# First operations of an attention and channel-mix kernel rearranged: loads on other queues, constants on another engine, a new order up to the first mixes

## The chip, the cores and the metric

The kernel runs on one core of a Trainium2 chip. The metric is the time of one execution on the device in microseconds, as a median of several runs. The core has five engines that each work through their own list of instructions in order and wait for one another by semaphores: TensorE (PE in the profile; its weight loads are PEld), VectorE (DVE), ScalarE (ACT), GpSimd (POOL) and SyncE (SP). SP, ACT and POOL also issue DMAs; an issue occupies the place in the issuing engine's list, and the data land later.

## The reference

Two layers in a row, for a batch of 8, 8 heads, 576 positions, head size 64:

```
def phi(x):                                   # x: q or k
    proj = x @ w_phi                          # 64 -> 128 features
    proj = proj - max(abs(proj), axis=-1)
    return concat([exp(proj), exp(-proj)])    # 256 features
q_p, k_p = phi(q), phi(k)
kv  = k_p^T v          ;  z = sum over positions of k_p
att = (q_p kv) / (q_p z + 1e-6)               # linear attention

x  = att, heads side by side                  # 8 x 576 x 512
xk = mu_k * x + (1 - mu_k) * x_prev           # x_prev: the position before
xr = mu_r * x + (1 - mu_r) * x_prev
k  = relu(xk @ w_k)                           # 512 -> 1024
out = sigmoid(xr @ w_r) * ((k * k) @ w_v)
```

Inputs and output are float32; the kernel computes with bfloat16 operands.

## The kernel before

**Tiles.** A batch is four pairs of heads; a pair has a number n from 0 to 31 (batch n // 4). Two heads of 64 partitions each fill the 128 partitions; a partition holds nine consecutive positions, so a pair's k is a tile of 128 x 576, and its q lies behind it in the same tile `nat` (1152 columns, nine groups of 128: groups 0 to 3 are k alone, group 4 is half k and half q, 5 to 8 are q alone).

**The operations, by their names in the code.** A number behind a name is the pair n, for loads and edges the batch and the first pair of the part.

- `hk`, `hq` (DMA issue), then `lk0.0.d`, `lq0.0.d` (cast to bf16): k and q of pair 0. `lk`, `lq`, `lv`: all other loads of k, q and v; k and q are cast by the DMA, which only GpSimd issues. `wphi`, `mus`, `wk`, `wr`, `wv`: the weights.
- `ones`, `ident`, `dve1`, `dve2`, `dve3`: constants. `ident` is the float32 identity (GpSimd); `dve3` makes its bf16 copy and the selection matrices `sel`; `dve1` casts `w_phi`; `dve2` fills thirteen buffers.
- `pt{n}.0`, `pt{n}.1`: transposes of `nat` on TensorE for batches 0 and 1; `pa{n}`, `pb{n}` copy the two halves from PSUM to `qkT`; `tr{n}` is done when both are. Later batches are transposed by DMA.
- `kp`, `qp`: projections on TensorE; `rk`, `rq`: VectorE's reduction to the largest absolute value; `ea`, `eb`: ScalarE's two exponentials of k; `em`: the small exponential of the maxima, which `va`, `vb` multiply into v.
- `mh`, `mt`, `mc`: the maxima of q, split in two bf16 parts, transposed and copied; `qt` makes the transposed projection minus the maximum, `qa`, `qb` its two exponentials.
- `kv`, `kc`: the product of k features and v, and its copy; `nd`: numerator and denominator; `ra`, `rd`: reciprocal and product.
- `xt`, `xe`, `xf`: attention output transposed and copied to `xs`; `df`: difference to the position before; `xa`, `xb`: the mixes with `mu_k` and `mu_r`.
- `tp`, `rt`, `mhe`, `mte`, `mce`, `eme`, `ekt`, `qte`, `eqe`: the same for the ninth group of each pair (the edge), for several pairs at once.
- `h`, `rl`, `sq`, `r`, `th`, `v`, `ob`, `so`: the channel mix of a batch, in eight blocks of `w_k` and four blocks of rows.

**What sets the order.** The string `ORDER` near the top lists all some 1500 operations; the program emits them in that order and every engine executes its own in it. `name:i` names the PSUM buffer (three of two banks, `P0` to `P2`, for most products; two of one bank, `M0` and `M1`, for the channel mix and transposes); `/ENGINE` names the engine where there is a choice; `+m@j` puts m filler matmuls of the constant `ones` into PSUM buffer j ahead of the operation, so that TensorE is not idle. Waits between engines follow from the data.

Batch 0 and most of batch 1's attention come first. The channel mix of batch 0 begins with `h0.0`, which needs the four mixes `xa0` to `xa3`; from there TensorE alternates between the channel mix of one batch and the attention of the next. The beginning of `ORDER` before:

```
ones hk hq ident dve2 hk.d hq.d wphi wphi.d lk0.1 lk0.1.d lq0.1 lq0.1.d mus mus.d lk0.2 lk0.2.d dve3
lq0.2 lq0.2.d lv0.0/POOL lv0.0.d lk0.0.d/DVE lq0.0.d/ACT lv0.1/SP lv0.1.d pt0.0:0+9@0 lv0.2/SP
lv0.2.d pt0.1:1 pa0/DVE pb0/ACT tr0 dve1 tp0.0:0+1@2 kp0:1 rt0.0 qp0:2 rk0 eme0.0 mhe0.0/POOL ekt0.0
```

Of the kernel before, what the change touches and what calls it, by code (L numbers as in the profile page):

```python
# [8 lines left out]
FP = mybir.dt.float32  # L9
# [10 lines left out]
ones hk hq ident dve2 hk.d hq.d wphi wphi.d lk0.1 lk0.1.d lq0.1 lq0.1.d mus mus.d lk0.2 lk0.2.d dve3  # L20
lq0.2 lq0.2.d lv0.0/POOL lv0.0.d lk0.0.d/DVE lq0.0.d/ACT lv0.1/SP lv0.1.d pt0.0:0+9@0 lv0.2/SP
lv0.2.d pt0.1:1 pa0/DVE pb0/ACT tr0 dve1 tp0.0:0+1@2 kp0:1 rt0.0 qp0:2 rk0 eme0.0 mhe0.0/POOL ekt0.0
pt1.0:1+1@0 lk1.0 lk1.0.d pa1/ACT mte0.0:0 rq0 ea0 lq1.0 lq1.0.d pt1.1:1+2@2 pb1/DVE tr1 lk1.2
lk1.2.d eb0 kp1:2+2@2 tp0.1:0 lq1.2 lq1.2.d rt0.1 em0 rk1 qp1:1+1@1 ekt0.1 mh0/POOL eme0.1 wk.0
wk.0.d mt0:1+1@1 mc0/ACT mce0.0/DVE rq1 ea1 qt0:0+1@2 wk.1 wk.1.d wk.d pt2.0:1 qa0 pt2.1:0
mhe0.1/DVE mh1/POOL pa2/DVE pb2/DVE tr2 eb1 vb0/POOL pt3.0:1+2@3 pt3.1:0 pa3/DVE qb0 pb3/DVE tr3
va0/POOL mte0.1:1+1@3 qp2:2 mt1:0 rq2 qp3:1 mce0.1/ACT mc1/ACT em1 qte0.1:1 wr.0 wr.0.d qt1:0 eqe0.1
qte0.0:0 rq3 lv1.0/POOL lv1.0.d qa1 tp0.2:2 va1/POOL qb1 rt0.2 kp2:1+3@1 rk2 vb1/POOL ekt0.2
kv0:0+1@1 eqe0.0 pt4.0:1 kc0/DVE ea2 mhe0.2/POOL pt4.1:0 pa4/DVE kp3:0 pb4/DVE tr4 kv1:2 wr.1 wr.1.d
wr.d eb2 rk3 pt5.0:0 wv.0 wv.0.d pt5.1:1 eme0.2 qp4:1 pa5/DVE kc1/ACT mh2/POOL em2 rq4 nd0:2  # L30
mh3/POOL pb5/ACT tr5 wv.1 wv.1.d wv.d em3 mt2:0 pt6.0:1 ea3 mc2/DVE ra0 nd1:1 vb2/POOL pa6/DVE rd0
eb3 pt6.1:0 pt7.0:1 va2/POOL pb6/DVE tr6 qt2:2 pa7/ACT ra1 rd1 mte0.2:0 qa2 lk2.0 lk2.0.d pt7.1:1
mce0.2/DVE qp5:0 pb7/DVE tr7 qte0.2:0 lq2.0 lq2.0.d qb2 rq5 tp1.0:1 xt0:1 va3/POOL eqe0.2 kv2:2
rt1.0 xf0/ACT xe0/ACT kp4:0 mh4/POOL mt3:0 kc2/ACT rk4 xt1:1 df0/POOL mc3/ACT ekt1.0 nd2:2 ra2 ea4
vb3/POOL xe1/DVE qt3:1+1@0 rd2 mt4:0 xf1/ACT mc4/ACT df1/DVE qa3 xt2:1 xa0 kv3:2 eb4 mhe1.0/DVE
xe2/DVE mte1.0:0+1@0 xb0 kc3/ACT kp5:0 qb3 qt4:2 xa1 eme1.0 xf2/DVE nd3:1 rk5 mce1.0/ACT df2/POOL
qa4 ra3 qb4 rd3 lv1.2/POOL lv1.2.d ea5 xa2 xt3:0+7@1 qp6:2 xb1 qte1.0:1 xe3/ACT qp7:1 eb5 xf3/DVE
df3/DVE xa3 em4 qt5:0+1@0 eqe1.0 rq6 vb4/POOL h0.0:0 qa5 va4/POOL rq7 kp6:2 qb5 h0.1:1 rk6 mh6/POOL
kp7:1 rl0.1/ACT kv4:0 va5/POOL rl0.0/ACT tr2.0 tr2.0.d tr8 tr9 mt6:1 kc4/DVE ea6 h0.2:0 rk7 vb5/POOL
eb6 xb2 kv5:0+1@2 mc6/ACT sq0.0/ACT xb3 nd4:2 tr2.2 tr2.2.d tr10 tr11 em6 ea7 h0.3:1 kc5/DVE  # L40
vb6/POOL ra4 rd4 nd5:0 eb7 vb7/POOL rl0.3/DVE qt6:2 rl0.2/ACT ra5 qp8:1 rd5 qa6 lv2.0/SP lv2.0.d
sq0.1/POOL r0.0:1 rq8 qb6 va6/POOL qp9:0 h0.4:0 rq9 th0.0 sq0.3/POOL sq0.2/ACT qt7:2 kv6:1 rl0.4/DVE
qa7 lk3.0 lk3.0.d tp2.0:0 kc6/DVE h0.5:1 mh8/POOL rt2.0 qb7 va7/POOL xt4:0 rl0.5/ACT kp8:1 xf4/DVE
xe4/DVE qp10:2 eme2.0 lq3.0 lq3.0.d r0.1:1 rk8 ekt2.0 mhe2.0/POOL r0.2:0 th0.1 rq10 sq0.4/POOL ea8
kp9:0 h0.6:1 rk9 lv2.2/POOL lv2.2.d eb8 kv7:2 th0.2 df4/DVE qp11:1 sq0.5/DVE rl0.6/ACT h0.7:0 xa4
em8 sq0.6/ACT kc7/DVE va8/POOL mt8:1 rq11 rl0.7/ACT nd6:2 mc8/ACT ea9 mte2.0:0 vb8/POOL xt5:1 ra6
nd7:1 rd6 tr3.0 tr3.0.d tr12 tr13 mce2.0/ACT eb9 vb9/POOL qte2.0:0 ra7 kv8:2 rd7 xf5/ACT sq0.7/ACT
qt8:0 va9/POOL kc8/DVE eqe2.0 kp10:1 xe5/DVE kp11:2 rk10 v0.0:1 tr3.2 tr3.2.d tr14 tr15 df5/POOL qa8
rk11 ea10 lk4.0 lk4.0.d v0.1:0 qb8 mh10/DVE xa5 lv3.0/SP lv3.0.d eb10 xb5 kv9:0 xb4 em10 qt9:1
kc9/ACT ob0.0 va10/POOL nd8:0 qa9 ob0.1 v0.2:1 qb9 vb10/POOL ra8 rd8 ea11 lq4.0 lq4.0.d mt10:0  # L50
tp3.0:0 ob0.2 kv10:1 mc10/ACT vb11/POOL eb11 rt3.0 so0.2 so0.2.d xt6:0 xt7:1 kc10/ACT va11/POOL
kp12:2 xf7/ACT xf6/DVE qt10:1 xe6/DVE ekt3.0 xz8 xz8.d xe7/DVE r0.3:0 df6/DVE qa10 rk12 df7/POOL
nd9:0 qb10 v0.3:1 ra9 mhe3.0/POOL rd9 th0.3 xa6 ea12 xz9 xz9.d mte3.0:0 qt11:0 xa7 eb12 nd10:1
mce3.0/DVE ob0.3 tr4.0 tr4.0.d tr16 tr17 h1.0:0 qa11 xb6 h1.1:1 qb11 ra10 xb7 kv11:2 rl1.0/ACT rd10
kp13:0 eme3.0 tr4.2 tr4.2.d tr18 tr19 sq1.0/POOL qte3.0:0 kc11/DVE rl1.1/ACT qp12:1 rk13 qp13:2
# [12 lines left out]
xz13 xz13.d qt16:1 kc15/ACT v1.3:1 xb11 ea17 tr5.2 tr5.2.d tr22 tr23 sqe0.0/DVE eb17 xa10 nd15:0
xa11 eme4.0 ve0:0 em16 ra15 ob1.3 qa16 va16/POOL so1.2 so1.2.d rd15 qb16 h2.0:1 va17/POOL obe0 xz14
xz14.d qp18:0 rl2.0/ACT qte4.0:0 vb16/POOL rq18 qp19:1 xz15 xz15.d eqe4.0 qp20:2 h2.1:1 sq2.0/POOL  # L70
rq19 so1.3 so1.3.d h2.2:0 rl2.1/ACT vb17/POOL rq20 sq2.1/ACT h2.3:1 lv4.2/SP lv4.2.d rl2.2/ACT soe0
soe0.d kp18:1 xb10 rl2.3/ACT kv16:2 sq2.3/ACT df12/DVE qp21:0 h2.4:1 xb12 sq2.2/ACT rq21 r2.0:0
rl2.4/ACT r2.1:1 th2.0 mh18/DVE kc16/DVE mh20/POOL xu13/ACT rk18 lk6.0 lk6.0.d kv17:0 th2.1 tp5.0:2
sq2.4/ACT lq6.0 lq6.0.d mt18:0 h2.5:1 rt5.0 kc17/ACT mc18/ACT df13/POOL ea18 mt20:0 nd16:0 mc20/DVE
rl2.5/DVE ekt5.0 h2.6:0 mhe5.0/POOL ra16 rd16 h2.7:1 eb18 sq2.5/DVE xz16 xz16.d xa13 qt17:0
rl2.6/ACT qt18:1 rl2.7/ACT sq2.6/DVE kp19:2 qa17 sq2.7/DVE r2.2:0 xb13 qa18 v2.0:1 xa12 xu14/ACT
rk19 th2.2 df14/POOL qb17 v2.1:0 ob2.0 xu15/ACT xa14 ea19 mte5.0:1 nd17:0 eme5.0 mce5.0/DVE ob2.1
eb19 v2.2:1 df15/DVE ra17 qb18 xa15 em18 qp22:2 ob2.2 qt19:1 vb18/POOL rq22 h3.0:0 tr6.0 tr6.0.d
tr24 tr25 qa19 va18/POOL r2.3:1 qb19 rl3.0/DVE rd17 vb19/POOL kp20:2 th2.3 qte5.0:0 kv18:1 rk20
# [81 lines left out]
def kernel(  # L161
# [17 lines left out]
    nc = tc.nc  # L179
# [102 lines left out]
    st = {}  # L282
# [734 lines left out]
```

## Time and profile before

| what | value |
|---|---|
| time, median of 3 runs | 285.27 us (283.28 to 286.0) |
| span of the profiled execution, first to last instruction | 275.3 us |
| median minus span | 10.0 us |
| TensorE busy | 261.7 us, 95% |
| VectorE busy | 234.6 us, 85% |
| ScalarE busy | 223.1 us, 81% |
| GpSimd busy | 142.4 us, 52% |

The profile lists the span of its execution, and no separate time for it; the runs shown are timed as a whole, and what lies around the span there is 10.0 us against the median. A line of the timeline has the start, the length, the engine, the line of code, the tile written and the tile read, and in brackets how long the engine was idle ahead of it and what ended that. Instructions of one engine overlap by up to about 0.1 us, so the cost of one is best read from its start to the start of the next.

### The profile page before, as it was taken

The page shows a single profiled execution, that of the slowest core. Times are in us where ns is not written, and L with a number is a line of the kernel's source. Part 1 is how long each engine was busy: PE and PEld are TensorE (multiplying, and loading weights), DVE is VectorE, ACT ScalarE, POOL GpSimd, SP SyncE. Part 2 cuts the span into 40 slices and gives each one's busy share as a digit, 9 for nine tenths or more (in the row PEclk, how much of TensorE's full clock was granted, in tenths as well). Part 3 has the DMA queues.
Part 4 walks back from the last instruction along what each step waited for, and adds up shares of the span by engine and source line. Part 5 has one row for each costly group of instructions (what it writes and reads, how often), then busy time and mean ns, then how long its engine had stood idle before and what let it go on. Part 6 is the DMA issues. An engine that isn't in the chain of part 4 may idle for free.

```text
span 275.3 us, 8865 instructions
## 1 busy us (share of the span) xinstructions
PE 261.7 (95%) x3682; PEld 154.1 (56%) x3730; DVE 234.6 (85%) x388; ACT 223.1 (81%) x413; POOL 142.4 (52%) x193
## 2 busy tenths in 40 slices
PE   7899889999899999999999999999999999999993
PEld 3567656566555566555565666555566565444542
DVE  6999999999799989999999889998889897864222
ACT  3899999999899997899898999789987777616330
POOL 5799557976818682633459465821931611300200
PEclk9999999999999999999999999999999999999999
DMA  7999999599999899759699998981725324142134
GB/s 147 285 209 250 209 213 174 114 235 175 238 129 200 202 219 185 155 127 248 99 166 164 215 249 142 171 255 41 161 89 88 77 52 100 42 110 67 29 88 116
DMA packets 65817, 42.89 MB, mean 156 GB/s; under 512 B 47152, under 2 KB 57008, under 8 KB 65776
## 3 DMA queue, kind: packets, MB, share of 16 engines
q1 hardware_dynamic: 54496, 27.54, 49.3%
q0 software_dynamic: 11056, 14.42, 29.1%
q8 instruction: 29, 0.48, 0.8%
q10 hardware_dynamic: 224, 0.36, 0.5%
q14 instruction: 12, 0.10, 0.1%
HBM read 33.62 MB, written 9.44 MB: 156 GB/s over the span
## 4 chain that ended last, share of the span: by engine, by line
PE 75%; DVE 8%; ACT 6%; issue 4%; DMA 3%; POOL 2%; SPq 0%; POOLq 0%; ACTq 0%
PE ps_h L810 19%; PE ps_v L843 17%; PE ps_r L829 9%; PE ps_nd L677 5%; PE ps_kv L656 5%; DMA qkT<-nat 3%; PE ps_he L897 3%; PE ps_ve L929 3%; PE ps_k L566 2%; PE ps_qT L630 2%; PE ps_q L566 2%; PE ps_qT L636 2%; ACT k L605 2%; DVE nmk L579 2%; PE ps_f L292 1%
## 5 line engine op out<-in xcount | busy, mean ns | idle before, releaser
L597 POOL TENSOR_TENSOR v<-vt,v 128x576 bf16<-128x576 f32 x59 | 69.8, 1203 | 33.5 <-ACT v L591 31.1
L605 ACT ACTIVATE k<-ps_k 128x1024 bf16<-128x1024 f32 x64 | 64.8, 1047 | 1.3 <-DVE nmk L579 1.3
L643 ACT ACTIVATE q<-ps_qT 128x1024 bf16<-128x1024 f32 x64 | 63.8, 1054 | 1.8 <-PE ps_qT L636 1.7
L810 PE MATMUL ps_h<-xk,wk_bf 128*128 128x512 bf16 x235 | 60.5, 380 | 1.2
L843 PE MATMUL ps_v<-wv_bf,kk 128*128 128x512 bf16 x244 | 58.2, 379 | 0.6
L579 DVE TENSOR_REDUCE nmk<-ps_k 128x8 f32<-128x1024 f32 x32 | 38.8, 1217 | 1.8 <-PE ps_k L566 1.5
L584 DVE TENSOR_REDUCE nmq<-ps_q 128x8 f32<-128x1024 f32 x32 | 38.3, 1217 | 1.6 <-PE ps_q L566 1.4
L843 PEld LDWEIGHTS <-kk 128*128 128x128 bf16 x256 | 24.1, 98 | 27.3
L810 PEld LDWEIGHTS <-wk_bf 128*128 128x128 bf16 x256 | 22.7, 97 | 25.0 <-issue 0.7
L206 ACT ACTIVATE krelu<-ps_h 128x512 bf16<-128x512 f32 x48 | 28.8, 611 | 9.3 <-PE ps_h L810 9.3
L726 POOL TENSOR_TENSOR diff<-xs 128x576 bf16<-128x576 bf16 x15 | 20.2, 1346 | 28.8 <-ACT xs L706 12.7
L214 POOL TENSOR_TENSOR kk<-krelu 128x512 bf16<-128x512 bf16 x18 | 19.1, 1068 | 30.3 <-ACT krelu L206 26.6
L849 DVE SCALAR_TENSOR_TENSOR ob<-rt,ps_v 128x512 f32<-128x512 bf16 x32 | 21.7, 682 | 14.3 <-PE ps_v L843 12.7
L829 PE MATMUL ps_r<-wr_bf,xr 128*128 128x512 bf16 x116 | 31.1, 380 | 0.7
L835 ACT ACTIVATE rt<-ps_r 128x512 bf16<-128x512 f32 x32 | 19.7, 615 | 8.8 <-PE ps_r L829 8.7
L732 DVE SCALAR_TENSOR_TENSOR xk<-diff,mu_k_t,xs 128x576 bf16<-128x576 bf16 x32 | 26.7, 839 | 0.1
L689 DVE TENSOR_TENSOR x_sc<-ps_nd,rden 128x640 bf16<-128x640 f32 x32 | 26.0, 817 | 0.6
L732 DVE SCALAR_TENSOR_TENSOR xr<-diff,mu_r_t,xs 128x576 bf16<-128x576 bf16 x32 | 25.6, 806 | 0.1
L656 PE MATMUL ps_kv<-v,k 64*128 64x65 bf16 x1024 | 22.4, 190 | 0.5 <-ACT q L643 0.2
L566 PEld LDWEIGHTS <-qkT 64*128 64x128 bf16 x512 | 16.5, 94 | 11.0 <-issue 8.0
L656 PEld LDWEIGHTS <-k 64*128 64x128 bf16 x1024 | 19.3, 94 | 5.7 <-issue 1.8
L677 PE MATMUL ps_nd<-kv,q 128*128 128x65 bf16 x512 | 21.4, 193 | 0.0
(102 smaller groups left out, 414.3 us busy)
## 6 DMA issues: line engine op xcount, KB each, us to landing
out_dram<-ob SPq DMA_DIRECT2D x70, 128.0 KB, 2.5
vt<-in_v_dram SPq DMA_DIRECT2D x11, 576.0 KB, 6.1
nat<-in_k_dram POOLq DMA_DIRECT2D x6, 576.0 KB, 7.8
nat<-in_q_dram POOLq DMA_DIRECT2D x6, 576.0 KB, 8.0
vt<-in_v_dram POOLq DMA_DIRECT2D x4, 576.0 KB, 6.0
wk_bf<-in_moe_w_k_dram POOLq DMA_DIRECT2D x2, 512.0 KB, 11.4
wv_bf<-in_moe_w_v_dram POOLq DMA_DIRECT2D x2, 512.0 KB, 10.6
nat<-in_k_dram POOLq DMA_DIRECT2D x3, 288.0 KB, 6.9
```

The costliest lines, as they stand in the source:

```text
L206: nc.scalar.activation(out_, in_, AF.Relu, scale=HALF)
L579: nc.vector.tensor_reduce(t[:, j, :], s["k"].rearrange("p a (g f) -> p (a g) f", f=128), axis=AX.X, op=ALU.max, apply_absolute_value=True, ...
L584: nc.vector.tensor_reduce(t[:, j, :], s["q"].rearrange("p a (g f) -> p (a g) f", f=128), axis=AX.X, op=ALU.max, apply_absolute_value=True, ...
L597: (nc.vector if eng == "DVE" else nc.gpsimd).tensor_tensor(vb[:, a, pn, :, 0:64], vt[b, a // 2][:, a % 2, :].rearrange("p (s d) -> p s d", ...
L605: nc.scalar.activation(s[f"k{pn}"], s["k"].rearrange("p a (g f) -> p (a g) f", f=128), AF.Exp, scale=(1.0 if pn == 0 else -1.0))
L643: nc.scalar.activation(t.rearrange("f x (a p) -> f x a p", a=2), s["qT"].rearrange("f a (x p) -> f x a p", p=64), AF.Exp, scale=(1.0 if pn ...
L656: nc.tensor.matmul(ps[:, hh, pn * 65:(pn + 1) * 65], lhsT=s[f"k{pn}"][r, c, :], rhs=vb[r, a, pn, 2 * g + par, :], start=(pn == 0 and c == ...
L677: nc.tensor.matmul(ps[:, bk, o * 65:(o + 1) * 65], lhsT=tail if sl < 2 else s[f"q{pn}"][:, 2 * G + h, :], rhs=s["kv"][:, h, pn, :], start= ...
L732: nc.vector.scalar_tensor_tensor(out=t[:, a, (b % 2) * S:(b % 2 + 1) * S], in0=s["d"], scalar=mu[:, a:a + 1], in1=xs[:, a, 0:S], op0=ALU.m ...
L810: nc.tensor.matmul(ps, lhsT=wk_bf[:, c, fc * 128:(fc + 1) * 128], rhs=xkt[bp][:, c, m0:m0 + 512], start=(c == 0), stop=(c == NDC - 1))
L829: nc.tensor.matmul(ps, lhsT=xrt[bp][:, c, m0 + ci * 128:m0 + (ci + 1) * 128], rhs=wr_bf[:, c, :], start=(c == 0), stop=(c == NDC - 1))
L843: nc.tensor.matmul(ps, lhsT=s["kk"][:, fc, ci * 128:(ci + 1) * 128], rhs=wv_bf[:, fc, :], start=(fc == 0), stop=(fc == NFC - 1))
```

## The change

The order is written anew from its first word to about `xf7`; from `r0.3` on it is the same. Up to `xa3` nearly all is in another place. The beginning of `ORDER` after:

```
ones hk wphi wphi.d wphj wphj.d dve2 hk.d ident dve0 lk0.0.d/DVE dve1 pt0.0:0+6@0 pa0/DVE kp0:1+1@2
rk0 hq hq.d lq0.0.d/ACT pt0.1:1 pb0/ACT lk0.1 lk0.1.d pt1.0:0 tr0 mus mus.d lq0.1 dve4 lq0.1.d lk0.2
lk0.2.d tp0.0:0+1@2 qp0:2 pa1/DVE rt0.0 rq0 pt1.1:1+1@0 ea0 ekt0.0 pb1/ACT tr1 kp1:0 qp1:2+1@1
pt2.0:1 dve3 rk1 lq0.2 lq0.2.d lv0.0/POOL lv0.0.d lv0.1/POOL lv0.1.d lk1.0 lk1.0.d lq1.0 mhe0.0/POOL
```

- `w_phi` is loaded in two halves from two queues (`wphi` on ACT's, `wphj` on SP's) in place of twice on SP's. `hq` goes from ACT's queue to SP's, behind `wphj`.
- The bf16 identity has an operation of its own (`dve0`), and the transposes wait for it and not for the rest of `dve3`, which now comes after the first reductions.
- The memsets of `xs` and `tq` (six) go from VectorE to GpSimd (`dve4`), behind the load `lq0.1`.
- The transposes of a pair are split 4 and 5 in place of 5 and 4: the first half holds k alone and waits only for k. The first projection of k (`kp`) waits for the first half alone.
- `mu_k` and `mu_r` are loaded as rows of 128 (two DMAs of 4 x 128), transposed on TensorE (`mut`) and copied by VectorE (`muc`); before, each was loaded column by column as 128 x 4 single elements.
- Both other loads of batch 0's v (`lv0.1`, `lv0.2`) go from SP's queue to GpSimd's.
- Some small operations change the engine: `mhe0.1`, `mhe1.0` from VectorE to GpSimd; `pb1`, `pa2`, `pa3`, `kc0`, `xf2`, `xf3` from VectorE to ScalarE; `pa1`, `pb5`, `mce0.1`, `mc1`, `xf0`, `kc3` from ScalarE to VectorE; `df0` and `df2` from GpSimd to VectorE, `df1` from VectorE to GpSimd.
- There are 29 filler matmuls in place of 36; the first group of them has 6 in place of 9.

```
-    def c_wphi():
-        for hh in range(2):
-            nc.sync.dma_start(out=wph_f32[64 * hh:64 * hh + 64, :], in_=w_phi)
+    def c_wphi(hh):
+        def f():
+            (nc.sync, nc.scalar)[hh].dma_start(out=wph_f32[64 * hh:64 * hh + 64, :], in_=w_phi)
+        return f
...
+    def c_dve0():
+        nc.vector.tensor_copy(ident, ident_f32)
     def c_dve2():
         for t in mhls + mhlts + [zero]:
             nc.vector.memset(t, 0.0)
+    def c_dve4():
         for t in xss:
-            nc.vector.memset(t[:, :, 0:1], 0.0)
+            nc.gpsimd.memset(t[:, :, 0:1], 0.0)
         for t in tqs[0] + tqs[1]:
-            nc.vector.memset(t[:, :, 0:64], 1.0)
+            nc.gpsimd.memset(t[:, :, 0:64], 1.0)
     def c_dve3():
-        nc.vector.tensor_copy(ident, ident_f32)
...
-                for g in range(5 * bk, min(R, 5 * bk + 5)):
-                    nc.tensor.transpose(pb[:, g - 5 * bk, :], nat[b][:, a, g * 128:(g + 1) * 128], ident)
+                for g in ((0, 1, 2, 3), (4, 5, 6, 7, 8))[bk]:
+                    nc.tensor.transpose(pb[:, g - 4 * bk, :], nat[b][:, a, g * 128:(g + 1) * 128], ident)
...
-                nc.scalar.dma_start(out=st["kq"][:, 1, :], in_=heads(q, 0, 0, 1)[:, 0, :])
+                nc.sync.dma_start(out=st["kq"][:, 1, :], in_=heads(q, 0, 0, 1)[:, 0, :])
...
-                    op(f"pt{i}.{bk}", "PE", 0.3, ("pt", i), pt(b, a, bk), [f"lk{tag}.d", f"lq{tag}.d", "dve3"],
+                    op(f"pt{i}.{bk}", "PE", 0.3, ("pt", i), pt(b, a, bk), [f"lk{tag}.d", "dve0"] + [f"lq{tag}.d"] * bk,
...
     def mus():
-        nc.sync.dma_start(out=mu_k_t, in_=moe_mu_k.rearrange("(c p) -> p c", p=128))
-        nc.sync.dma_start(out=mu_r_t, in_=moe_mu_r.rearrange("(c p) -> p c", p=128))
+        for i, mu in enumerate((moe_mu_k, moe_mu_r)):
+            nc.sync.dma_start(out=mu_rows[NDC * i:NDC * i + NDC, :], in_=mu.rearrange("(c p) -> c p", p=128))
+    def mut():
+        st["mu"] = ps = motile(("mo", "mu"), "ps_mu")
+        nc.tensor.transpose(ps[:, 0:2 * NDC], mu_rows, ident_f32[0:2 * NDC, 0:2 * NDC])
+    def muc():
+        nc.vector.tensor_copy(mu_t, st["mu"][:, 0:2 * NDC])
...
-        op("kp" + N, "PE", 0.23, (K("kp"), n), kp, ["tr" + N, "dve1"],
+        op("kp" + N, "PE", 0.23, (K("kp"), n), kp, [("pa" if b < NPT else "tr") + N, "dve1"],
```

## The prediction

> **What bounds the kernel now.** I read the page first, then the windows by stage, then the timelines of ScalarE and VectorE up to the first block of the channel mix.
>
> ```profile
> span 275.3 us, 8865 instructions
> ...
> PE 261.7 (95%) x3682; PEld 154.1 (56%) x3730; DVE 234.6 (85%) x388; ACT 223.1 (81%) x413; POOL 142.4 (52%) x193
> ```
>
> ```profile
> 35.00:40.00 5.00, 4.53 (x55) 2.52 (x53) 4.89 (x9) 5.00 (x10) 2.45 (x3) 1.00 1.11 249
> 40.00:60.00 20.00, 19.06 (x346) 11.39 (x351) 19.84 (x28) 19.65 (x36) 16.59 (x22) 1.00 0.88 159
> ...
> 100.00:150.00 50.00, 49.42 (x740) 28.42 (x747) 47.75 (x74) 43.18 (x80) 27.64 (x36) 1.00 0.92 164
> ```
>
> The columns are TensorE, weight loads, VectorE, ScalarE, GpSimd, clock, DMA share and GB/s. Behind 40 us TensorE is full (49.4 of 50 us). Ahead of it ScalarE and VectorE are full, and TensorE's time is padded with fillers. The new order ends there, so the question is how much earlier `h0.0` and the blocks behind it start (39.61 us here); what is won or lost by then should arrive at the end one to one.
>
> ```profile
> 4.83 0.67 ACT L200 CAST nat<-kk 128x576 bf16<-128x576 f32 x1 [2.37 <-DMA kk<-in_q_dram]
> 6.54 0.59 ACT L200 COPY qkT<-ps_pt 128x512 bf16<-128x512 bf16 x1 [1.03 <-PE ps_pt L338]
> ...
> 8.84 1.95 ACT L605 ACTIVATE k<-ps_k 128x1024 bf16<-128x1024 f32 x2
> ...
> 11.87 0.27 ACT L200 COPY mT<-ps_m 128x128 bf16<-128x128 bf16 x1 [0.34 <-PE ps_m L620]
> ...
> 19.80 1.94 ACT L605 ACTIVATE k<-ps_k 128x1024 bf16<-128x1024 f32 x2 [0.20 <-DVE nmk L579]
> ...
> 39.95 2.06 ACT L643 ACTIVATE q<-ps_qT 128x1024 bf16<-128x1024 f32 x2
> 42.28 1.08 ACT L206 ACTIVATE krelu<-ps_h 128x512 bf16<-128x512 f32 x2 [0.27 <-PE ps_h L810]
> ```
>
> From `ea0` at 8.84 to `qa5` at 39.95 ScalarE is idle for 0.34 + 0.20 us only. Its first `krelu` then waits 0.27 us for TensorE, so ScalarE is not the very last there; VectorE is:
>
> ```profile
> 4.67 0.46 DVE L202 CAST nat<-kk 128x576 bf16<-128x576 f32 x1 [0.62 <-DMA kk<-in_k_dram]
> 6.26 0.49 DVE L202 COPY qkT<-ps_pt 128x640 bf16<-128x640 bf16 x1 [1.13 <-PE ps_pt L338]
> ...
> 8.68 1.22 DVE L584 TENSOR_REDUCE nmq<-ps_q 128x8 f32<-128x1024 f32 x1
> 9.81 0.41 DVE L202 COPY qkT<-ps_pt 128x512 bf16<-128x512 bf16 x1
> ...
> 39.61 2.35 DVE L584 TENSOR_REDUCE nmq<-ps_q 128x8 f32<-128x1024 f32 x2
> ```
>
> `xa3` ends where `rq6` starts, at 39.61. Of these 39.6 us VectorE is busy for 35.5; of the 4.1 idle, 3.0 lie ahead of `rk0` (7.55) and 1.1 behind it.
>
> **The start.** Here the change does most. k's cast begins at 4.67, as its data land 3.9 us after the issue at 0.74; q's ends at 5.50, and only then the transposes begin (5.53), behind nine fillers that last 4.02 us.
> - k's landing: 4.65 as now if its own queue limits it, or about 3.5 if it no longer shares the engines with q (by the DMA rates of the first microseconds 288 KB have moved by 3.2). I take 4.0. Cast 0.46: 4.5. Six fillers (6 x 0.43) end at 4.03. Four transposes (now five in 0.70): 5.1. `dve1` lies ahead of `pa0` on VectorE and waits for both halves of `w_phi`; SP's lands at 1.21 + 3.8 = 5.0, as the first one now, and before the second one now (1.80 + 4.4). `pa0` 0.4: 5.6. `kp0` to `rk0` 0.45, `rk0` 1.13: **7.25, now 8.68**.
> - q is issued third on SP, at 1.80 and not at 0.74. It lands at 5.0 if the bytes decide (the same bytes are ahead of it as now), at 5.9 if 4.1 us from the issue stay; I take 5.3. Cast 0.67, five transposes 0.65, `pb0` 0.69: 7.3. `ea0` is behind it on ScalarE: **7.3, now 8.84**. `tp0.0` and `qp0` need `pb0`, so `rt0.0` starts at 7.7 and `rq0` ends at **9.3, now 9.81**.
>
> The Trainium skill has a rule against fewer fillers. "TensorE: Matmul & The Clock Gate", Part 1, says that the array runs at half its clock until about 3.4 us of sustained activity. The rows: fillers 0.43 us apart up to 4.42, the first five transposes in 0.70 us, later ones in 0.45, so the gate opens near 5.6, some 4.1 us behind the first matmul. (The page's clock row shows 9 throughout and does not show this.) Six fillers are 2.6 us. By the row the gate opens at the same time and only `pt0.0` is slow, which is in the sum; by the rule, with TensorE pausing at 4.0, `kp0` (8) and `pt0.1` (5) are slow too, 13 x 0.053 = 0.7 us on the two paths together. I keep the row; 0.7 goes into the range.
>
> **ScalarE's sum.** Behind `ea0` it has 31.11 - 0.54 = 30.57 us of work up to `qa5`. `eme0.0` (0.20), `ekt0.0` (0.39) and `pb1` (0.58) come behind `ea0` now: +1.17. Engine changes: `pa2`, `pa3` +0.92, `kc0` +0.26, `xf2`, `xf3` +0.20; `kc3` -0.26, `mce0.1`, `mc1` -0.30, `pb5` -0.46, `pa7` (four groups in place of five) -0.19, `xf0` -0.10: +0.07. So 31.8, from 7.3: 39.1, and with the same 0.54 idle **39.65, now 39.95: -0.3 us**. Most of the 1.5 won at `ea0` is work that was done in the gap ahead of it.
>
> **VectorE's sum.** At the end of `rq0` it is 0.5 ahead. But `dve3` without the identity (2.89 to 4.05, 1.16 us) was done in the wait for k and is now among the reductions; `pa1` is done in place of `pb1` (-0.4). The rest of the list: `mhe0.1`, `mhe1.0` -0.54, `pa2`, `pa3` -0.66, `kc0` -0.33, `df1` -0.38, `xf2`, `xf3` -0.30; `pb5` and wider `pb7` +0.47, `kc3` +0.35, `df0`, `df2` +0.76, `mce0.1`, `mc1` +0.26, `xf0` +0.12, `muc` +0.13: -0.12. Together +0.64 - 0.5 = **+0.1 us** at the same 1.1 idle. The six memsets (1.8 to 2.8) also leave VectorE, but they lay in its wait for k; that gains nothing.
>
> **GpSimd and the loads.** `dve4` is not in the trace on GpSimd. Bounds: 1.1 us as on VectorE, or 1.6 by GpSimd's 0.20 for 128 float32 columns (four of 256 at most 0.4); I take 1.4. It is hidden in GpSimd's idle 2.95 us ahead of 7.70, but `lk0.2` behind it is issued at 4.1 and not 2.69, `lq0.2` at 4.85 and not 3.40, and `pt2.0` stands on TensorE at about 10 in place of 12.65. Behind that two v issues (+1.4) and `mhe0.1`, `mhe1.0` (+0.9) against `df0` or `df2` (-1.3) leave it about 1 us more up to `vb3`. Then `vb3` ends near 30, ahead of `kv3` (31.67 now).
>
> ```profile
> nat<-in_k_dram POOLq DMA_DIRECT2D x3, 288.0 KB, 6.9
> nat<-in_q_dram POOLq DMA_DIRECT2D x3, 288.0 KB, 7.8
> ...
> kk<-in_k_dram SPq DMA_DIRECT2D x1, 288.0 KB, 3.9
> ...
> mu_k_t<-in_moe_mu_k_dram SPq DMA_DIRECT2D x1, 2.0 KB, 7.1
> mu_r_t<-in_moe_mu_r_dram SPq DMA_DIRECT2D x1, 2.0 KB, 8.5
> ```
>
> The two `mu` loads are 1024 packets of 4 bytes; while they run the DMA engines stay full and the rate falls from 380 to 60 GB/s (6 us). As rows they are eight packets of 512 bytes, and two v loads leave SP's queue as well. So I let the loads of pairs 1 to 3 land no later than now plus their later issue: `lk0.2` 4.1 + 6.4 = 10.5, `lq0.2` 4.85 + 7.8 = 12.6. `pa2` on ScalarE is due at about 10.7; nothing large is lost. `mut` is one small transpose where TensorE has room. Seven fillers fewer cost nothing where TensorE waits anyway.
>
> **The sum.** ScalarE -0.3, VectorE +0.1 at equal idle. The idle behind `rk0` (0.2, 0.2, 0.3 for TensorE's projections) may shrink by 0.3 to 0.5, as projections stand earlier in the list. I take **-0.3 us: 285.0**, from a span of 275.3 to 275.0 with the 10.0 us around it.
>
> **Rivals.**
> - **The gaps close.** q lands at 5.0 (-0.3), ScalarE loses its 0.54 and VectorE its 1.1. ScalarE then sets it: 39.95 to 38.8, -1.15: **284.1**. For it: both are full but for these gaps, and the small `mu` packets go. Against: each gap has its own cause, and a new order has new ones.
> - **The loads come late (slower).** `pt2.0` and `pt2.1` stand early in TensorE's list and block all behind them. Take the longest landings for 288 KB in the first 13 us, 8.6 for k and 9.3 for q: `lk0.2` lands at 12.7, `pa2` starts at 13.2, and ScalarE is idle 2.5 us: 0.3 less 2.5 is +2.2, **287.5**. It decides from `lk0.2` landing after about 10.5. For it: later issue, earlier use. Against: fewer bytes and packets ahead.
> - **The start is no earlier.** The order does what it says, but k lands at 4.65, q at 5.9 and TensorE is cold: `ea0` at about 8.2, +0.6: **285.9**.
>
> **How the numbers follow.** The forecast has 0.5, closed gaps 0.23, late loads 0.17, no earlier start 0.10. A measurement of this kernel tells about 1% (2.9 us) from no change; the three runs shown spread from -0.7 to +0.3%. Over 1% faster needs more than closed gaps: 0.14, from that case and scatter. Over 1% slower: 0.13, most of the late loads with a second stall. Within: 0.73. The range reaches from closed gaps with scatter, 282.5, to late loads, 287.5.
>
> **What would show it.** Right: `rk0` ends near 7.3, `ea0` starts near 7.3, `rq0` ends near 9.3, ScalarE without idle from there to `qa5` near 39.6; `h0.0` between 39 and 40. Wrong: a ScalarE copy `qkT` between 9 and 14 us with over 1 us of idle behind `ps_pt` (late loads); `h0.0` before 38 (the gaps were worth more, or the sums missed work); or a span that differs by more than `h0.0` does, which would mean that what lies behind 40 us is not the same.

## The result, and the profile after: 1.2% slower, and in the profile a start that is 6 us later

| | before | after |
|---|---|---|
| median of 22 executions each | 284.6 us | 284.19 us |
| lowest and highest | 279.5 to 290.68 us | 281.83 to 297.93 us |
| time against before, as a ratio | 1 | 1.0116, 95% interval 1.0068 to 1.0164 |
| span of the profiled execution | 275.3 us | 281.4 us |
| `h0.0` starts | 39.61 us | 45.64 us |

The ratio leaves out executions that lie more than 1.5% above the fastest of their kernel, and this is why it can show a loss where the medians are equal. What makes so many executions of before long is found below (e8 and e9).

The page of after, cut to the lines that answer to those of before, and the row of the granted clock:

```profile
span 281.4 us, 8854 instructions
...
PE 263.6 (94%) x3675; PEld 154.9 (55%) x3724; DVE 234.8 (83%) x380; ACT 224.0 (80%) x413; POOL 143.8 (51%) x204
...
PEclk9599979999999999999999999999999999999999
```

The work is what it was (VectorE 234.8 us, ScalarE 224.0); the span is 6.1 us longer. The clock row has a 5 and a 7 in its second and sixth slice, where before had 9 throughout. The windows by stage of after (TensorE, weight loads, VectorE, ScalarE, GpSimd, granted clock, DMA share, GB/s) show where:

```profile
4.80:8.20 3.40, 0.66 (x10) 0.22 (x8) 1.65 (x2) 0.40 (x1) 2.93 (x5) 0.97 1.05 167
8.20:11.60 3.40, 3.01 (x25) 2.06 (x26) 1.54 (x3) 2.34 (x5) 0.51 (x3) 0.50 1.13 275
11.60:15.00 3.40, 3.03 (x27) 1.63 (x26) 2.91 (x6) 2.37 (x6) 3.30 (x6) 0.52 1.19 217
...
35.40:38.80 3.40, 2.23 (x53) 1.44 (x54) 2.25 (x5) 3.40 (x6) 1.71 (x2) 0.99 1.16 175
38.80:42.20 3.40, 3.18 (x34) 2.02 (x35) 3.35 (x6) 2.26 (x5) 0.25 (x1) 0.51 1.19 223
...
100.00:150.00 50.00, 49.38 (x727) 29.20 (x732) 47.49 (x76) 44.35 (x83) 24.43 (x34) 1.00 0.93 173
```

From 4.8 to 8.2 us TensorE works for 0.66 us and ScalarE for 0.40. In the two stretches behind it TensorE is busy again, at half the clock, and a second time from 38.8 to 42.2 us (clock 0.51). From 100 to 150 us TensorE is as full as before (49.38 of 50 us, before 49.42), and from `h0.0` to the end both kernels take the same: 281.4 - 45.64 = 235.8 us, before 275.3 - 39.61 = 235.7. The loss of this profile is made ahead of `h0.0`.

What stands still is seen on the timelines of ScalarE and of VectorE:

```profile
7.80 0.67 ACT L200 CAST nat<-kk 128x576 bf16<-128x576 f32 x1 [5.21 <-DMA kk<-in_q_dram]
9.28 0.69 ACT L200 COPY qkT<-ps_pt 128x640 bf16<-128x640 bf16 x1 [0.81 <-PE ps_pt L348]
9.87 1.03 ACT L624 ACTIVATE k<-ps_k 128x1024 bf16<-128x1024 f32 x1
...
46.48 1.05 ACT L662 ACTIVATE q<-ps_qT 128x1024 bf16<-128x1024 f32 x1
```

```profile
3.81 0.46 DVE L202 CAST nat<-kk 128x576 bf16<-128x576 f32 x1 [1.90 <-DMA kk<-in_k_dram]
...
5.81 1.22 DVE L598 TENSOR_REDUCE nmk<-ps_k 128x8 f32<-128x1024 f32 x1 [0.50 <-PE ps_k L585]
9.71 0.42 DVE L202 COPY qkT<-ps_pt 128x512 bf16<-128x512 bf16 x1 [2.68 <-PE ps_pt L348]
...
10.91 1.22 DVE L603 TENSOR_REDUCE nmq<-ps_q 128x8 f32<-128x1024 f32 x1
...
45.74 2.36 DVE L603 TENSOR_REDUCE nmq<-ps_q 128x8 f32<-128x1024 f32 x2
```

k is early: its cast starts at 3.81 (before 4.67) and `rk0` at 5.81 (before 7.55). q is late: its cast starts at 7.80 (before 4.83), and ScalarE has waited 5.21 us for that DMA alone. `pt0.1` needs q, and it stands ahead of `pt1.0` in TensorE's list, so TensorE waits too, and then VectorE for TensorE (2.68). `ea0` starts at 9.87 (before 8.84). The list of DMA issues of the first 6 us (line, queue, kind, count, KB, us to landing) shows which loads lie together:

```profile
kk<-in_k_dram SPq DMA_DIRECT2D x1, 288.0 KB, 3.1
kk<-in_q_dram SPq DMA_DIRECT2D x1, 288.0 KB, 5.9
...
nat<-in_k_dram POOLq DMA_DIRECT2D x1, 144.0 KB, 5.8
nat<-in_q_dram POOLq DMA_DIRECT2D x1, 144.0 KB, 6.3
```

q is issued on SP at 1.84, third on its queue, and takes 5.9 us; on ACT's queue, issued at 0.74 beside k, it took 4.1. The two cast loads of pair 1 (`lk0.1`, `lq0.1`, issued by GpSimd at 1.44 and 2.15) are under way in the same microseconds, and take 5.8 and 6.3 where before they took 4.4 and 5.4. The packets of the two queues from 4.9 to 5.3 us (packets, MB, share of the 16 DMA engines' time; q0 carries GpSimd's cast loads, q1 SP's loads):

```profile
q0 software_dynamic: 32, 0.03, 53.5%
q1 hardware_dynamic: 30, 0.07, 50.2%
```

Here q goes packet for packet with the cast loads, and has half of the engines' time.

The second stretch at half clock delays the mixes as well. The same sixteen products of an `nd` take 1.07 us in after, and 0.67 in e10 below, whose start is the same. First after, then e10:

```profile
38.96 1.07 PE L696 MATMUL ps_nd<-kv,q 128*128 128x65 bf16 x16
```

```profile
37.95 0.67 PE L696 MATMUL ps_nd<-kv,q 128*128 128x65 bf16 x16
```

From the filler ahead of it, at 37.07 (36.78 in e10), to `h0.0` after needs 8.57 us and e10 7.27: 1.3 us of the 6.0 are lost here. Of the nine profiles with the new start, after's and eight below, only after and e1 have this stretch. In the 3.4 us ahead of it TensorE is busy for 2.2 us and never idle for more than 0.55 us at once; what sets it off stays open.

### The profile page after: what moved, and what is told of

Its sections match the earlier page's. It is cut to its first block, busy times and chain, and to the rows that moved or that the text cites. A ratio compares the mean times of both kernels' runs of the same rounds, so it can differ in the third digit from the quotient of the medians.

```text
span 281.4 us, 8854 instructions
## 1 busy us (share of the span) xinstructions
PE 263.6 (94%) x3675; PEld 154.9 (55%) x3724; DVE 234.8 (83%) x380; ACT 224.0 (80%) x413; POOL 143.8 (51%) x204
## 4 chain that ended last, share of the span: by engine, by line
PE 79%; ACT 6%; DMA 5%; DVE 4%; issue 2%; POOL 2%; SPq 0%; ACTq 0%; DVEq 0%; POOLq 0%
PE ps_h L829 19%; PE ps_v L862 18%; PE ps_r L848 10%; PE ps_nd L696 6%; PE ps_kv L675 5%; DMA qkT<-nat 3%; PE ps_he L916 3%; PE ps_k L585 3%; PE ps_qT L649 3%; PE ps_ve L948 3%; PE ps_q L585 2%; PE ps_qT L655 2%; DMA kk<-in_q_dram 2%; DVE nmq L603 2%; ACT k L624 2%
## 5 line engine op out<-in xcount | busy, mean ns | idle before, releaser
L598 DVE TENSOR_REDUCE nmk<-ps_k 128x8 f32<-128x1024 f32 x32 | 38.8, 1218 | 3.7 <-PE ps_k L585 3.2
L745 POOL TENSOR_TENSOR diff<-xs 128x576 bf16<-128x576 bf16 x14 | 18.7, 1338 | 26.9 <-ACT xs L725 12.8
L751 DVE SCALAR_TENSOR_TENSOR xk<-diff,mu_t,xs 128x576 bf16<-128x576 bf16 x32 | 26.6, 839 | 0.1
L751 DVE SCALAR_TENSOR_TENSOR xr<-diff,mu_t,xs 128x576 bf16<-128x576 bf16 x32 | 25.7, 808 | 0.1
```

The costliest lines, as they stand in the source:

```text
L598: nc.vector.tensor_reduce(t[:, j, :], s["k"].rearrange("p a (g f) -> p (a g) f", f=128), axis=AX.X, op=ALU.max, apply_absolute_value=True, ...
L751: nc.vector.scalar_tensor_tensor(out=t[:, a, (b % 2) * S:(b % 2 + 1) * S], in0=s["d"], scalar=mu[:, a:a + 1], in1=xs[:, a, 0:S], op0=ALU.m ...
```

## The experiments

Theory from the two traces: q's late landing and the cold TensorE behind it are the 6 us. Rivals: TensorE's clock alone; the queue that q is on; the new order itself, with gaps of its own. Later a second question came up: why executions of one kernel lie 277 to 290 us apart.

**e1: q on ACT's queue, as before.** In the order:

```
-ones hk wphi wphi.d wphj wphj.d dve2 hk.d ...   -rk0 hq hq.d lq0.0.d/ACT ...
+ones hk hq wphi wphi.d wphj wphj.d dve2 hk.d ...   +rk0 hq.d lq0.0.d/ACT ...
```

and `nc.scalar` in place of `nc.sync` for q.

> The changed kernel, but q of pair 0 is issued first on ACT's queue (ahead of w_phi's half), as before the change. Theory 1 (q's late landing holds TensorE's list at pt0.1): q lands near 4.8 in place of 7.8, ea0 starts near 7.0 in place of 9.9, TensorE's clock stays full behind 8 us, the channel mix begins 3 to 5 us earlier (41 to 43 us), and the span falls by as much, to 276.5 to 278.5. Rival (the new order behind the start is the worse one): ea0 moves as above but the channel mix still begins at 44 us or later and the span stays within 1.5 us of 281.4.

Measured: ratio to before 1.0053 (1.0016 to 1.009), median 281.29 us. The timelines of ScalarE and VectorE of this kernel:

```profile
4.73 0.67 ACT L200 CAST nat<-kk 128x576 bf16<-128x576 f32 x1 [1.67 <-DMA kk<-in_q_dram]
7.63 0.69 ACT L200 COPY qkT<-ps_pt 128x640 bf16<-128x640 bf16 x1 [2.23 <-PE ps_pt L348]
```

```profile
5.73 0.23 DVE L254 CAST wph<-wph_f 128x128 bf16<-128x128 f32 x1 [0.71 <-DMA wph_f<-in_w_phi_dram]
```

q's cast starts at 4.73, 3.1 us earlier, but `pb0` only at 7.63. Now the halves of `w_phi`, one of them behind q on ACT's queue, land at 5.3 and 5.6 (4.0 and 4.1 in after): `dve1` waits for them, `pa0` behind it on VectorE, `kp0` for `pa0`, and `pt0.1` behind `kp0` on TensorE. q in time gives 1.6 us at `ea0` (8.25) and 2.6 at `h0.0` (43.09), not all; the second stretch at half clock is in this trace too (36.35 to 39.77 us).

**e2: q second on SP's queue, `w_phi`'s half third.** Only the order: `hk hq wphi wphi.d wphj wphj.d`, and `rk0 hq.d`.

> The changed kernel, but q of pair 0 is issued second on SP's queue, ahead of w_phi's half and not behind it (0.6 us earlier, same queue). If the place among the loads decides (q comes to the DMA engines before the two cast loads of pair 1), q lands near 5 and the span is as in the run with q on ACT's queue. If SP's queue itself carries one load of k's size at a time, q lands near 7 and half of the loss stays.

Measured: ratio 1.0127 (1.0051 to 1.0203), median 282.1 us. q landed 3.3 us behind its issue, and the half of `w_phi` behind it took 5.0: `pb0` at 8.63, `h0.0` at 43.18. A load of 32 KB in third place is late as one of 288 KB is, and both orders put something there that TensorE's list needs.

**e3: `dve4` ahead of the cast loads `lk0.1` and `lq0.1` on GpSimd.** q stays third on SP.

```
-... hk.d ident dve0 lk0.0.d/DVE ...   lq0.1 dve4 lq0.1.d lk0.2
+... hk.d ident dve4 dve0 lk0.0.d/DVE ...   lq0.1 lq0.1.d lk0.2
```

> The changed kernel, but GpSimd's six memsets come ahead of the two cast loads of pair 1 (lk0.1, lq0.1), which are issued 1.1 to 1.3 us later; q stays third on SP's queue. If q is late because it shares the DMA engines with these two loads, it lands near 5.5 and ea0 starts near 7.7; pair 1 comes later, so the span gains 1 to 3 us. If q is late because of its own queue, it still lands after 7.3.

Measured: ratio 1.003 (0.998 to 1.008), median 280.98 us. The cast loads are issued at 2.31 and 3.02, 0.9 us later than in after. One line of the DMA issues, and two of ScalarE's timeline:

```profile
kk<-in_q_dram SPq DMA_DIRECT2D x1, 288.0 KB, 4.0
```

```profile
5.83 0.67 ACT L200 CAST nat<-kk 128x576 bf16<-128x576 f32 x1 [3.23 <-DMA kk<-in_q_dram]
...
7.63 1.03 ACT L624 ACTIVATE k<-ps_k 128x1024 bf16<-128x1024 f32 x1
```

From the same place on the same queue q takes 4.0 us in place of 5.9. So the place alone is not what costs: it costs when one cast load is issued 0.4 us ahead of q and the next 0.3 us behind it (1.44 and 2.15 against 1.84), and not when both come behind: from 4.0 to 4.5 us SP's queue moves 71 packets beside 9 of the cast loads. The other profiles say the same: with the cast loads as in after q takes 5.9 to 6.1 us (after, e4, e10, e11), with both behind it 3.6 and 4.0 (e12, e3). `ea0` is at 7.63 and `h0.0` at 40.94, 4.7 us earlier than in after, by moving one word in the order; against e10 and e11 below, which have no second stretch at half clock, it is 3.1 and 2.4 us.

**e4: ten more fillers ahead of `pt0.1`** (`pt0.1:1+10@2`), so that TensorE works while q is late.

> The changed kernel with ten filler matmuls more, ahead of pt0.1, so that TensorE is busy while q is awaited. If the half clock from 8 to 15 us is a large part of the loss, the clock stays above 0.9 there and the span falls by 1 to 2.5 us from 281.4. If q's landing alone costs the time, the clock is full but the span stays within 0.7 us of 281.4 (or rises where the fillers are still running when q has landed).

Measured: ratio 1.0069 (1.0022 to 1.0115), median 281.08 us. q's cast is as late as ever (7.78), but `h0.0` starts at 42.55. Two rows of TensorE's timeline in e4, the nine transposes (`pt0.1` and `pt1.0`) and the filler behind them:

```profile
8.51 0.68 PE L348 MATMUL ps_pt<-ident,nat 128*128 128x128 bf16 x9 [0.26 <-ACT nat L200]
9.02 0.38 PE L302 MATMUL ps_g<-ones 128*128 128x512 bf16 x1
```

and the same two in after:

```profile
8.53 1.14 PE L348 MATMUL ps_pt<-ident,nat 128*128 128x128 bf16 x9 [2.77 <-ACT nat L200]
9.47 0.63 PE L302 MATMUL ps_g<-ones 128*128 128x512 bf16 x1
```

The same nine transposes, started within 0.02 us of each other, take 0.68 us in one and 1.14 in the other. A pause of 2.8 us behind 4.3 us of fillers, transposes and products (1.46 to 5.77) makes TensorE slow for what follows. `h0.0` is 3.1 us earlier than in after; 1.4 of these are the second stretch, which e4 does not have (7.17 us from the filler at 35.38 to `h0.0`, 8.57 in after). So the first is worth about 1.7 us here, and 1.5 and 0.8 against e10 and e11.

**e5: e1 and e3 together.**

> The changed kernel with two repairs at once: q of pair 0 first on ACT's queue, and GpSimd's memsets ahead of the cast loads of pair 1. If the late start is what the change lost, k, q and both halves of w_phi land by about 5, ea0 starts at 6.5 to 7.5, the clock stays full, and the channel mix begins at 39.5 to 41 us: a span of 275 to 277, level with the kernel before or faster. If the new order behind the start has more gaps of its own, ea0 starts that early too, but the mix begins 33 us or more behind ea0 (30.8 before the change) and the span stays above 277.

Measured: five of six executions at 290 to 295 us, the sixth at 278.26. At the start q's cast was at 5.17 and k's at 5.00 (both loads, side by side, took 4.2 and 4.4 us), `ea0` at 8.56, `h0.0` at 41.88: no better than e3. Behind it TensorE stood still for 10.76 us in one wait, at about 74 us, for a DMA transpose. That made the second question.

**e6: before, with q on SP's queue behind `w_phi`.** `hk ident dve2 hk.d wphi wphi.d hq hq.d`, and `nc.sync` for q.

> The kernel before, with one part of the change: q of pair 0 is issued last of four on SP's queue, behind both loads of w_phi, and no longer on ACT's. Theory 1: q lands 2 to 3 us later (7 to 8 us), the transposes, which need k and q there, start as late, and the span rises by 2.5 to 6 us, the more so if TensorE's clock falls in the pause. Rival (the place of q costs little, the order is what costs): the span stays within 1 us of 275.3.

Measured: ratio 1.0411 (1.0306 to 1.0516), median 290.07 us. The late q is here as well (cast 7.75, TensorE at a clock of 0.53 from 8.2 to 11.6), and costs the old order 3.5 us at `h0.0` (43.15). Most of the rest is again the wait at 74 us, 9.22 us here.

**e7: before, with `mu_k` and `mu_r` loaded as rows** (`mut`, `muc` as in after, behind `tr3`).

> The kernel before, with mu_k and mu_r loaded as rows, transposed and copied as in the change, and nothing else. If the 1024 packets of 4 bytes slow the other loads, lk0.2 and lq0.2 land 1 us or more earlier than 6.4 and 7.8 us after their issue and the dip of the DMA rate between 5 and 7 us goes; the time stays within 0.5%, as nothing waits for these loads. If the dip has another cause, it stays.

Measured: ratio 1.0173 (0.9955 to 1.0391) from four executions, which tells nothing of the time. The trace tells enough: `lk0.2` and `lq0.2` landed 7.1 and 9.4 us behind their issue, with the packets of 4 bytes 6.4 and 7.8. The loads came no sooner, and `h0.0` was at 39.99.

**e8: before, unchanged, beside e5 to e7.**

> The kernel before, unchanged, with a profile of its own: how far the one profiled execution of before (275.3 us, clock full throughout) stands for its runs. If it does, most undisturbed runs have spans of 275 to 278 and a clock of 1.0; if it was a good draw, they lie at 277 to 281 with clocks below 1.0.

Measured: median 281.78 us, 278.71 to 291.43; ratio to the other executions of the same kernel 1.0074 (0.9965 to 1.0183). `h0.0` at 39.78 as in the profile of before, and a span that is 4.4 us longer. So the profiled execution of before (275.3) was one of its fastest, and 4.2 us of another lie behind `h0.0`.

2.8 of them lie in one wait, and TensorE is at half clock for 3.4 us behind it (75.18 to 78.59). The one that waits is the first product of batch 3's edge (`tp3.0`, tile `ps_e`) and it waits for the second of batch 3's two DMA transposes. Its row in TensorE's timeline, in before, in e8 and in e6:

```profile
71.63 0.29 PE L466 MATMUL ps_e<-wph,qkT 64*128 64x128 bf16 x4 [1.07 <-DMA qkT<-nat]
```

```profile
74.54 0.28 PE L466 MATMUL ps_e<-wph,qkT 64*128 64x128 bf16 x4 [3.82 <-DMA qkT<-nat]
```

```profile
83.75 0.39 PE L466 MATMUL ps_e<-wph,qkT 64*128 64x128 bf16 x4 [9.22 <-DMA qkT<-nat]
```

Four transfers meet here. GpSimd issues `lq3.0` and, 10.3 us later in before, `lk4.0`, whatever happens. SP may start batch 3's first transpose (`tr3.0`) only when `lq3.0` has landed, and the second (`tr3.2`) 3.0 to 3.6 us behind it. Put side by side, over the kernels so far, in the order of the lead, which runs from the start of `tr3.2` on SP to the issue of `lk4.0` on GpSimd (all columns are from the same traces):

| kernel | `lq3.0` lands after | lead of `tr3.2` | `tr3.2` lands after | TensorE's wait |
|---|---|---|---|---|
| e1 | 6.2 us | 1.2 us | 8.4 us | 1.0 us |
| e4 | 6.4 | 1.1 | 7.2 | 0 |
| after | 6.2 | 0.9 | 8.2 | 1.0 |
| e3 | 6.4 | 0.9 | 9.4 | 2.2 |
| e2 | 6.2 | 0.9 | 7.1 | 0 |
| before | 6.1 | 0.5 | 7.8 | 1.1 |
| e8 | 6.7 | 0.3 | 10.4 | 3.8 |
| e7 | 6.7 | 0.3 | not recorded | 6.3 |
| e5 | 7.2 | 0.0 | 17.2 | 10.8 |
| e6 | 7.3 | -0.2 | 15.7 | 9.2 |

Where `lq3.0` lands 1 us later than in before (e5, e6), TensorE waits 8 to 10 us longer; among the kernels with a lead of 0.9 us the wait still differs, from 0 to 2.2 us. Where the transpose loses its lead, SP needs 6.0, 7.8 and 7.2 us to issue it (e5, e6 and e11 below), in before 3.5. In e6 the DMA engines are not full meanwhile (columns as above; 0.42 is their busy share, 29 the GB/s):

```profile
72.00:74.00 2.00, 2.00 (x25) 1.14 (x22) 1.83 (x4) 2.00 (x3) 2.00 (x3) 1.00 0.42 29
```

A table of what goes together shows no cause, so the next four runs moved `lk4.0`, the transfer at the end of the chain.

**e9: before, `lk4.0` one GpSimd operation later.**

```
-... df5/POOL qa8 rk11 ea10 lk4.0 lk4.0.d v0.1:0 ... ob0.0 va10/POOL nd8:0 ...
+... df5/POOL qa8 rk11 ea10 v0.1:0 ... ob0.0 va10/POOL lk4.0 lk4.0.d nd8:0 ...
```

> The kernel before with one load moved: lk4.0 (batch 4's k, 576 KB, a cast load on GpSimd) stands behind va10 in the order instead of behind df5. Theory A (a race of two transfers): lk4.0 is issued a fixed 10.3 us behind lq3.0 on GpSimd, while batch 3's two DMA transposes (SP) start only when lq3.0 has landed, 6.1 to 7.3 us behind its issue, and the second starts 3.1 to 3.6 us behind the first. In the profiles so far the second transpose's lead over lk4.0 and its landing time go together: lead 0.9 to 1.2 us, landing in 7.1 to 9.4 us and TensorE's wait at ps_e 0 to 2.2 us; lead 0.3 to 0.5, landing 7.8 to 10.4 and more, wait 1.1 to 6.3; lead 0 or less, landing 15.7 to 17.2, wait 9.2 to 10.8. Moved behind va10, lk4.0 is issued some 4 us later: lead over 4 us, landing under 8 us, wait at most 1 us in every execution; h0.0 at 39.6 to 40; the slow half of the executions vanishes: median 277 to 279 us where before has 282 to 284, spread under 5 us; ratio of the undisturbed runs about 0.99. Theory B (the spread is the chip's: the clock or the memory's): the wait at ps_e and the spread of 277 to 290 us stay, median 282 to 284. What could spoil A: lk4.0 and lq4.0 then land close behind one another, and tr4.0 at about 79 us may wait for them, up to 3 us.

Measured: median **278.09 us**, lowest 277.48, highest 279.45 in 16 executions, where 47 executions of before on the same chip had 283.2 (277.25 to 289.71). Ratio 0.9902 (0.9872 to 0.9932). `lk4.0` is issued at 68.85, 5.3 us behind the start of `tr3.2`. How long the two transposes took to land (least, median, longest), in e9 and in before:

```profile
DMA to landing us min/median/max: 5.2/5.8/6.4
```

```profile
DMA to landing us min/median/max: 6.5/7.1/7.8
```

The wait at `ps_e` is gone and the spread of 12 us is 2. Theory A held; what could have spoiled it, `tr4.0` waiting for the later load, shows as a start at 80.30 in place of 78.84 and cost little, as the median tells.

**e10: after, with the same move.**

> The kernel after with the same move of lk4.0 behind va10. In the profiled execution of after the lead of the second transpose was 0.94 us and the wait 1.0 us, so less is to be had than from before: theory A: h0.0 at 45.5 as in after, wait at ps_e 0 to 1 us, median 281 to 283 us, and against e9 the whole of the start's 6 us shows: 2.1% longer than e9, where after against before showed only 1.2%, because half of the executions of before lose several us in this race and those of after fewer. Theory B: median 284, and e10 to e9 the same 1.2%.

Measured: median 281.55 us (280.49 to 286.88, 22 executions), ratio to before 1.0083 (1.0054 to 1.0112). Freed of the race, after is 3.5 us, 1.2%, behind e9 by the medians. I had expected the whole 6 us; in this profile `h0.0` starts at 44.05, not 45.64.

**e11: after, `lk4.0` one operation sooner (ahead of `df5`).**

> The kernel after with lk4.0 one GpSimd operation sooner (ahead of df5, 1.27 us). Theory A: the lead of the second transpose turns from 0.94 us to about -0.3 us, it lands in 15 to 17 us, TensorE waits 9 to 11 us at ps_e and half-clock windows follow: nearly every execution at 290 to 294 us. Theory B (lead and landing only happen to go together): as after, 282 to 285 us.

Measured: median 288.5 us (285.72 to 292.56), ratio 1.0288 (1.0213 to 1.0363). `lq3.0` landed after 6.1 us, as in the good cases; still `tr3.2`, with a lead of -0.5 us, took 11.3 us, and TensorE waited 4.02. The sign is as theory A has it, but the transpose lands in 11.3 us and not 15 to 17, and TensorE's wait is less than half of what I took from e5 and e6. So the lead alone makes the transpose late, with `lq3.0` in time; that the two late loads of e5 and e6 cost more has a cause beside it, which is open.

**e12: e3 with `lk4.0` behind `va10`.**

> The kernel of e3 (after with dve4 ahead of lk0.1 and lq0.1 on GpSimd, so that q lands in time) with lk4.0 behind va10 as in e9. Theory A: h0.0 at 41 as in e3, wait at ps_e 0 to 1 us, median 278 to 280 us with a spread under 5 us; 1.3 us behind e9, which is what the new order of the start costs by its own gaps even with q in time. Rival: with q in time the new order of the start is as good as the old: e12 equal to e9 within 0.3 us.

Measured: median 278.29 us (277.12 to 283.73, 16 executions), ratio 0.9913 (0.9864 to 0.9961). `ea0` at 7.24, `h0.0` at 40.02. By the median it is 0.2 us behind e9: here the rival was right, and the new start is as good as the old when q is in time. Its spread is wider than e9's: six of the 16 executions are longer than e9's longest. e9 and e12 both beat the two kernels of this case.

## Why the prediction was wrong

It said 285.0 us from 285.27, within 1% of no change. The median of after, 284.19 us, lies in the range; the change against before does not: 1.2% slower, and by none of the rivals named.

- **k and `rk0`.** k landed at 3.8 (taken: 4.0), `rk0` ended at about 6.95 (7.25). Held, a little better. So did `dve4`: 1.2 us on GpSimd (taken: 1.4), and `lk0.2` issued at 3.74 (4.1).
- **q's landing, the step that failed.** Taken as 5.3, between 5.0 (same bytes ahead) and 5.9 (4.1 us from the issue); it was 7.78. The first bound counted the bytes ahead of it, the second kept its time from the issue. Neither counted GpSimd's two cast loads, which the same move put level with q: q's issue went from 0.74 to 1.84, behind that of `lk0.1` (1.44). The trace of before had q ahead of them, so no row showed it; e3 did. `ea0` was at 9.87 in place of 7.3. In e12, with both cast loads behind q, q landed at 5.42, `ea0` started at 7.24 and `h0.0` at 40.02, close to what was forecast (5.3, 7.3, and 39 to 40).
- **The clock: the pause was priced too low, and the row was misread.** I weighed the Trainium skill, "TensorE: Matmul & The Clock Gate", Part 1, against the rows of before and kept the row. The transposes of before are 0.107 us apart up to 6.13 us and 0.056 behind it, so there the full clock came at 6.2 us and not at 5.6; in after it came at 4.61. `kp0`, slow by the rule as I applied it, took 0.40 us in after, at full pace. What was slow lay behind the pause, which neither reading had at its length: `pt0.1` and `pt1.0` took 1.14 us against 0.68, and fillers 0.63 against 0.38. And the price was wrong too: I counted 13 instructions at 0.053 us, 0.7 us, where nearly all of TensorE's work from 8.5 to 14.8 us is slow and three engines wait for it; against e4 that is 0.8 to 1.7 us, and 1.3 more for the second stretch, which the prediction did not have at all. The page also says that the window in which TensorE's activity is counted runs freely, so that the number of slow matmuls differs from run to run; after, e10 and e11, whose start is the same, agree: their first full clock is at 4.61, 13.80 and 4.96 us.
- **ScalarE's sum from `ea0` to `qa5`.** Taken: 31.8 us and 0.54 idle. In e12, with q in time, it is 40.84 - 7.24 = 33.6 us, with 1.2 idle: work 0.6 more than my list has, idle 0.7 more. In after it is 36.6, with 3.8 idle. "Equal idle" was a guess on an order that had not run; it holds to about 1 us where the start is right and fails by 3 where it isn't.
- **`mu` as rows.** The claim that the packets of 4 bytes held the other loads back fell with e7, by its one trace.
- **One to one from `h0.0` to the end.** Held in the profiles: 235.7 and 235.8 us. It does not hold from one execution to the next, because of the race at `tr3.2`, and I didn't ask what a shift by some us does to transfers that start by different clocks.
- **"10.0 us around the span."** Each run lists its span, and the time around it is 283.14 - 281.4 = 1.7 us. The profiled execution of before took about 277 us and was one of its fastest, so the sum was made from a base that few executions reach. It cancels in the forecast of a difference.
- **The rivals.** "Start no earlier" had q at 5.9 and a cold TensorE, in the right place, and priced the two together at +0.6 us, a tenth of what they were. "Loads late" looked at `lk0.2` (landed at 9.9) and not at q.

**The account.** Of the 6.0 us at `h0.0` in the profiled execution, 1.3 are the second stretch at half clock. Without it (e10, e11) `h0.0` is at 44.05 and 43.30, 4.4 and 3.7 us behind before. Of these 3.1 and 2.4 go when q is in time (e3), 1.5 and 0.8 when TensorE is merely kept busy (e4), and of what e3 leaves, 1.3 us, only 0.2 to 0.4 are left in e12. In the medians without the race it is 3.5 us (e10 against e9). Among kernels with the same start `h0.0` differs, as TensorE was slow for different lengths: 45.64, 44.05 and 43.30 us in after, e10 and e11. Against before as it is, the ratio gives 1.16%, some 3.2 us of 280. The plain medians show nothing of it (284.6 and 284.19), for executions of before lose some us at `tr3.2`: lift that out, and its median falls from 283.2 to 278.1 (e9), that of after from 284.19 to 281.55 (e10). The lead was 0.5 us in the profile of before and 0.9 in that of after, whose GpSimd is 0.3 us slower from `lq3.0` to `lk4.0` (10.64 us against 10.33); that this is why after loses less is argued from those numbers, not tested alone.

What stays open: what sets off the second stretch at half clock, and why two transfers at once in e6 move 29 GB/s. The Trainium skill, "DMA: Bandwidth & Descriptors", section "Queues, rings and completion order", says that each DMA engine takes turns between queues packet by packet. The packets of after agree with it for q (30 of SP's queue beside 32 of the cast loads). For e6 turns are not enough: the engines' busy share is 0.42 there.

## What to carry to other kernels

When a load is moved to another queue, list everything on all queues that is then issued ahead of it or within a microsecond, and price its landing against those, not against its own queue; and see which engine's in-order list stands behind it. A TensorE that pauses for some 3 us in its first ten paid for the pause twice here. Where executions of one kernel spread by 4%, compare two of their traces before anything else: here one wait, and one word in the order, were worth more than the whole change.

## What the runs showed of the hardware that was not expected

- A DMA transpose that starts 0.5 to 1.2 us ahead of a cast load of 576 KB lands in 7 to 9.4 us (before, after, e1 to e4), one that starts 0.3 us ahead in 10.4 (e8), one that starts with it or behind it in 11 to 17 us (e5, e6, e11), and with the cast load 5 us away in about 5.3 us (e9, e10, e12).
- The entries of TensorE's granted clock in the traces change only at whole multiples of 3.41 us from the first one: in after full at 4.61, half at 8.03, full at 14.85, half at 38.75, full at 42.16 us. The first full clock came at 4.6 to 7.2 us in ten of the 14 profiles, and at 9.05, 10.79, 9.35 and 13.80 us in e1, e2, e5 and e10, where TensorE had paused for 0.9 to 2.6 us ahead of it.
- A granted clock of 1.00 in a window can mean that the trace has no entry for it. In e10 the first entry is at 13.80 us; the window below, ahead of it, reads 1.00, and in it the nine transposes take 1.14 us and a filler 0.63 us, the slow durations. The durations of equal matmuls are the better witness. First the window, then the rows of TensorE's timeline, both of e10:

```profile
8.20:11.60 3.40, 2.85 (x24) 1.89 (x25) 1.38 (x3) 2.50 (x5) 0.37 (x2) 1.00 1.12 266
```

```profile
8.69 1.14 PE L348 MATMUL ps_pt<-ident,nat 128*128 128x128 bf16 x9 [2.63 <-ACT nat L200]
9.63 0.63 PE L302 MATMUL ps_g<-ones 128*128 128x512 bf16 x1
```
